# An attention backward loop emitted from two block programs, with dK and dV one unit later and three score banks in turn

## The chip, the cores and the metric

The kernel runs on one core of one Trainium2 chip. All times are device microseconds (us) of that core, from the first to the last instruction. One profiled execution of each kernel gives the trace; the times come from several executions. The engines are PE (TensorE: matmuls), ACT (ScalarE), DVE (VectorE) and POOL (GpSimd). The granted clock is the share of PE's full clock that the trace records as granted; a halving is a change of it from 1.0 to 0.5.

## The reference, cut to what matters

The program is a forward pass and the full vector-Jacobian product of one block: layer norm with modulation, attention with 32 heads of width 16 over 2048 tokens, then an MLP. Only the backward pass of the attention is touched:

```python
B, S, D, H = (1, 2048, 512, 32)                     # Dh = D // H = 16
def _A_ref(x, wqkv, wo):
    qkv = (x @ wqkv).reshape(B, S, 3, H, Dh).transpose(2, 0, 3, 1, 4)
    q, k, v = (qkv[0], qkv[1], qkv[2])
    scores = jnp.einsum('bhqd,bhkd->bhqk', q, k) * Dh ** (-0.5)
    p = _softmax(scores, axis=-1)
    o = jnp.einsum('bhqk,bhkd->bhqd', p, v)
    return o.transpose(0, 2, 1, 3).reshape(B, S, D) @ wo
# ... layer norms, modulation, MLP; then
_out, _vjp = jax.vjp(_f, A_x, A_wqkv, A_wo, B_w1, B_b1, B_w2, B_b2, c, w_mod)
_grads = _vjp(grad_out)
```

## The kernel before

The backward loop has 512 units. A unit is four heads, 128 queries and 512 keys; four units are a block. Per unit PE makes four scores (a 32-row tile of the array each), ACT their exponentials E, PE four products psD (32-row tiles again), DVE the two dS products, and PE a K quad and a V quad (four matmuls in four 32-column tiles, into accVK). dS is transposed by DMA, except for one unit in eight, whose tile is turned on PE and copied by ACT. After every sixteen units ACT copies accVK out (the vkb copy). Per block sixteen matmuls (dqacc) make dQ. All engines but POOL run in the order in which the loop emits.

```python
ework = ...tile_pool(name="phIe", bufs=4)            # E_u and dS_u
psd = ...tile_pool(name="psId", bufs=2, PSUM)        # psD, two banks each
pss = ...tile_pool(name="psIs", bufs=2, PSUM)        # two score banks
psx = ...tile_pool(name="psIx", bufs=1, PSUM)        # px (shared) and accVK

def score(u, hq, shared):                            # cut
    r = 32 * hq
    psS = psx.tile(..., tag="px") if shared else pss.tile(..., tag="ps")
    PE.matmul(psS[:], st["q"][r:r + 32, qt*P:(qt+1)*P], st["k"][r:r + 32, kc*512:kc*512+512],
              start=True, stop=True, tile_position=(r, 0))
    ACT.activation(bst[u][0][:, hq, :], psS[:], AF.Exp, scale=SCALE)

def k_quad(u):                                       # v_quad alike, with E_u and dOs_tok
    for hq in range(4):
        PE.matmul(cur["vk"][32*hq:32*hq+32, :], hst[hg]["qz"][:, qt, hq, :], bst[u][1][:, hq, :],
                  start=(qt == 0), stop=False, tile_position=(0, 32*hq), skip_group_check=True)

for j in range(2 * NU + 15):                         # half units
    u, pair, sub = j // 2, j % 2, j % 8
    for hi in range(2):
        i = 2 * sub + hi
        score(u, 2*pair + hi, i == 1 or (i in (4, 7) and not (j >= 8 and on_pe(j // 8 - 1))))
    if "turn" in held: ...                           # ACT copies the turned tile
    dp_pair((j - 1) // 2, (j - 1) % 2)               # two psD matmuls, one dS product on DVE
    if (j - 1) % 2 == 1: transpose_unit((j - 1) // 2)
    if 2 <= u < NU + 2:
        (k_quad if pair == 0 else v_quad)(u - 2)     # one quad in every half unit
    if sub in (1, 3) and on_pe(b): pe_turn(b, sub // 2)
    if sub in (5, 6): ...                            # two dq quads each
```

## Time and profile before

| | before |
|---|---|
| median time | 2749.24 us (3 runs, 2740.08 to 2750.76) |
| span of the profiled run | 2744.2 us |
| backward loop, first to last dS product | 1327.4 us, of 64 repeats of two blocks |
| mean granted PE clock, whole span | 0.897 |

The prediction below shows the slices, the loop's stretch, the groups and the timelines that it rests on. The first is the clock row of the page's 40 slices of before (tenths of the full clock); the second is a row of the groups, with busy time and mean ns behind the bar, then the idle time before it and what ended it:

```profile
PEclk8655569998998999787999999999999999999999
L1056 PE MATMUL psD_u<-iv,ido 32*128 32x512 bf16 x2048 | 406.6, 393 | 20.1 <-DMA ido<-dOT_st 14.3 <-DVE dS_u L1058 5.0
```

From slice 19 on, inside the loop, the clock is 9 tenths or more everywhere. In the stages ahead of it it is lower in places. A psD matmul then has a mean duration of 393 ns.

### The profile page before, as it was taken

How to read it: one execution, taken by the hardware profiler on the slowest of the kernel's cores; microseconds unless marked ns; L12 is line 12 of the kernel's file. 1: busy time of each engine (PE TensorE's matmuls, PEld its weight loads, DVE VectorE, ACT ScalarE, POOL GpSimd, SP SyncE). 2: the span in 40 equal slices, each digit the busy share in tenths (PEclk: the TensorE clock that was granted, in tenths of full speed). 3: DMA queues.
4: the chain of work that ended last, by engine and by line, in shares of the span. 5: the costliest groups of instructions: out<-in, count | busy, mean ns of one | idle time of the engine just before them, and what ended most of it. 6: DMA issues, size and time to landing. Idle time of an engine off the chain costs nothing.

```text
span 2744.2 us, 48487 instructions
## 1 busy us (share of the span) xinstructions
PE 2383.2 (87%) x18010; PEld 781.8 (28%) x18010; DVE 1763.4 (64%) x2232; ACT 2304.7 (84%) x3537; POOL 379.1 (14%) x378
## 2 busy tenths in 40 slices
PE   6799989888988988586898988988888989888899
PEld 2211123222322222232332333333233232332343
DVE  7101144435345443356988989989999898998973
ACT  4599999999999998202999999999999899998953
POOL 2000010211333133201011110101101011010100
PEclk8655569998998999787999999999999999999999
DMA  9863365346847656786999999999999999999982
GB/s 241 197 177 92 102 147 132 107 116 142 116 83 161 139 95 138 170 226 161 187 179 195 192 194 192 192 195 188 196 193 189 189 190 193 188 188 206 184 247 81
DMA packets 1271906, 459.69 MB, mean 168 GB/s; under 512 B 1152739, under 2 KB 1240807, under 8 KB 1271414
## 3 DMA queue, kind: packets, MB, share of 16 engines
q1 hardware_dynamic: 1254262, 425.42, 77.6%
q0 software_dynamic: 10944, 16.78, 4.2%
q10 hardware_dynamic: 6464, 14.40, 1.9%
q8 instruction: 142, 2.33, 0.3%
q14 instruction: 94, 0.77, 0.1%
HBM read 97.67 MB, written 74.47 MB: 63 GB/s over the span
## 4 chain that ended last, share of the span: by engine, by line
PE 27%; ACT 20%; DMA 4%; DVE 3%; issue 3%; SPq 1%; ACTq 1%; POOL 0%; DVEq 0%; POOLq 0%
ACT E_u L1046 15%; PE psS_u L1044 10%; PE accVK L1098 3%; ACT dsT L1157 3%; PE accVK L1089 3%; DVE dS_u L1058 2%; PE ptT L1079 2%; PE dqacc L1116 2%; PE pdh L1284 2%; PE pwq L1318 2%; DMA dsT<-dS_u 1%; PE psS_x L1044 1%; ACT dqtmp L1126 1%; PE psD_u L1056 1%; DMA part<-p_st 1%
## 5 line engine op out<-in xcount | busy, mean ns | idle before, releaser
L1058 DVE TENSOR_TENSOR dS_u<-psD_u,E_u 128x1024 bf16<-128x1024 f32 x1024 | 1196.4, 1217 | 146.8 <-PE psD_u L1056 88.9
L1046 ACT ACTIVATE E_u<-psS_u 128x512 bf16<-128x512 f32 x1790 | 990.8, 619 | 102.9 <-PE psD_u L1056 53.6
L701 ACT ACTIVATE ET<-psST 128x1024 bf16<-128x1024 f32 x1024 | 944.4, 1299 | 38.7 <-PE psST L699 37.7
L1044 PE MATMUL psS_u<-ik,iq 32*128 32x512 bf16 x1790 | 618.0, 386 | 106.2 <-ACT E_u L1046 64.7
L699 PE MATMUL psST<-qt_sb,kt_sb 32*128 32x512 bf16 x2048 | 408.3, 464 | 64.9 <-ACT ET L701 31.2
L1056 PE MATMUL psD_u<-iv,ido 32*128 32x512 bf16 x2048 | 406.6, 393 | 20.1 <-DMA ido<-dOT_st 14.3
L715 PE MATMUL oacc<-ET,vaug 128*32 128x512 bf16 x2048 | 247.5, 474 | 6.0 <-DVE ostage L719 6.0
L1044 PEld LDWEIGHTS <-iq 32*128 32x128 bf16 x2048 | 121.0, 91 | 342.2 <-issue 315.8
L1089 PE MATMUL accVK<-dS_u,qz 128*32 128x512 bf16 x2048 | 209.6, 398 | 3.0 <-DVE dS_u L1058 0.2
L1098 PE MATMUL accVK<-E_u,dOs_tok 128*16 128x512 bf16 x2048 | 205.4, 391 | 0.0
L699 PEld LDWEIGHTS <-kt_sb 32*128 32x128 bf16 x2048 | 90.0, 94 | 399.7 <-issue 388.6
L1131 POOL TENSOR_TENSOR dQacc<-dQacc,dqtmp 128x512 f32<-128x512 f32 x64 | 81.1, 1268 | 884.6 <-ACT dqtmp L1126 876.8
L1056 PEld LDWEIGHTS <-ido 32*128 32x128 bf16 x2048 | 105.1, 91 | 265.4 <-issue 262.4
L1046 ACT ACTIVATE E_u<-psS_x 128x512 bf16<-128x512 f32 x258 | 160.0, 620 | 14.8 <-PE psS_u L1044 14.6
L1116 PE MATMUL dqacc<-dsT,KS_tok 128*32 128x512 bf16 x2048 | 159.8, 390 | 12.2 <-ACT dsT L1157 12.2
L719 DVE COPY ostage<-oacc 128x512 f32<-128x512 f32 x32 | 22.0, 688 | 229.9 <-PE oacc L715 210.7
L376 DVE COPY part<-pm 128x512 f32<-128x512 f32 (+2 forms) x105 | 64.6, 615 | 150.7 <-PE pm L362 128.1
L1157 ACT ACTIVATE dsT<-ptT 128x1024 bf16<-128x1024 bf16 x128 | 134.4, 1050 | 1.1 <-PE ptT L1079 1.0
L715 PEld LDWEIGHTS <-vaug 128*32 128x32 bf16 x2048 | 54.9, 96 | 163.8 <-issue 163.8
L1044 PE MATMUL psS_x<-ik,iq 32*128 32x512 bf16 x258 | 100.4, 389 | 0.6 <-ACT E_u L1046 0.6
L1079 PE MATMUL ptT<-identb,dS_u 128*128 128x128 bf16 x1024 | 81.3, 224 | 11.6 <-ACT dsT L1157 11.4
L1089 PEld LDWEIGHTS <-qz 128*32 128x32 bf16 x2048 | 55.4, 93 | 123.3 <-issue 121.0
(262 smaller groups left out, 2104.1 us busy)
## 6 DMA issues: line engine op xcount, KB each, us to landing
p_st<-part POOLq DMA_DIRECT2D x36, 256.0 KB, 5.6
kt_sb<-qkT_st SPq DMA_DIRECT2D x128, 64.0 KB
wA<-in_B_w_dram SPq DMA_DIRECT2D x28, 256.0 KB
wB<-w1T_st SPq DMA_DIRECT2D x28, 256.0 KB
dsT<-dS_u SPq DMA_TRANSPOSE x448
wA<-w2T_st SPq DMA_DIRECT2D x21, 256.0 KB
wB<-in_B_w_dram SPq DMA_DIRECT2D x21, 256.0 KB
p_st<-part POOLq DMA_DIRECT2D x27, 192.0 KB, 4.2
```

What stands on the lines that cost most here:

```text
L699: PE.matmul(ps[:, hi, :], kt_sb[r:r + 32, kt * P:(kt + 1) * P], qt_sb[r:r + 32, :], start=True, stop=True, tile_position=(r, 0))
L701: ACT.activation(ET[:, 2 * pair:2 * pair + 2, :], ps[:], AF.Exp, scale=SCALE)
L715: PE.matmul(oacc[32 * hq:32 * hq + 32, :], lhsT, ET[:, hq, :], start=(kt == 0), stop=(kt == TT - 1), tile_position=(0, 32 * hq), skip_grou ...
L1044: PE.matmul(psS[:], st["q"][r:r + 32, qt * P:(qt + 1) * P], st["k"][r:r + 32, kc * 512:kc * 512 + 512], start=True, stop=True, tile_positi ...
L1046: ACT.activation(bst[u][0][:, hq, :], psS[:], AF.Exp, scale=SCALE)
L1056: PE.matmul(psD[:, hi, :], st["do"][r:r + 32, qt * P:(qt + 1) * P], st["v"][r:r + 32, kc * 512:kc * 512 + 512], start=True, stop=True, til ...
L1058: DVE.tensor_tensor(dS_u[:, 2 * pair:2 * pair + 2, :], psD[:], E_u[:, 2 * pair:2 * pair + 2, :], ALU.mult)
L1079: PE.transpose(pt[:, i, :], held["dS"][:, 2 * half + i // 4, kt * P:(kt + 1) * P], identb[:])
L1089: PE.matmul(cur["vk"][32 * hq:32 * hq + 32, :], hst[hg]["qz"][:, qt, hq, :], bst[u][1][:, hq, :], start=(qt == 0), stop=False, tile_positi ...
L1098: PE.matmul(acc[32 * hq:32 * hq + DH, :], dOs_tok[:, qt, (hg * 4 + hq) * DH:(hg * 4 + hq + 1) * DH], E_u[:, hq, :], start=False, stop=(qt ...
L1116: PE.matmul(acc[32 * hq:32 * hq + 32, :], KS_tok[:, kc * 4 + kt, h * DH:h * DH + 32], tT[:, :, hq * 4 + kt, :], start=(kt == 0), stop=(kt ...
L1157: ACT.activation(dst, pt[:], AF.Identity)
```

## The change

The intent was to take three waits out of the loop: scores that wait for exponentials (a third bank for every score), dS products that wait behind the dK/dV work (quads one unit later), and dS products that wait for the transposing DMA (a fifth E and dS buffer). For that the loop over half units became two strings of marks, one for blocks that turn a tile on PE and one for the others: `s` score, `e` exponential, `D` psD pair with its dS product, `q` a K or V quad, `t`/`T` turn and copy, `d`/`Q` dQ matmuls and their copy out.

```diff
-        ework = ph.enter_context(tc.tile_pool(name="phIe", bufs=4))
+        ework = ph.enter_context(tc.tile_pool(name="phIe", bufs=5))
-        pss = ph.enter_context(tc.tile_pool(name="psIs", bufs=2, space=bass.MemoryType.PSUM))
+        banks = {"A": "ps0", "B": "ps1", "C": "px"}
     ... (score and expo become two functions, dq_out is split from dq_quad)
+        order_t = (
+            "s0 q s1 e0 e1 D s2 q s3 e2 D s4 q e3 s5 s6 D "
+            "e4 e5 t1 q e6 s7 D s8 T1 s9 e7 e8 s10 e9 D s11 e10 "
+            "t2 q e11 T2 s12 e12 s13 D e13 D q d1 d2 s14 D Q s15 "
+            "e14 q q e15 ").split(), "ACBACBAABCABABBA"
+        order_n = (
+            "q s0 e0 s1 D q s2 e1 D e2 s3 q s4 e3 D s5 d1 "
+            "e4 e5 d2 s6 D s7 Q q q e6 e7 q s8 e8 D s9 q "
+            "e9 s10 s11 D e10 q e11 s12 e12 s13 D e13 s14 s15 D e14 e15 ").split(), "CBACBABACBACBACB"
-            for j in range(2 * NU + 15):
-                ... (one fixed program, one quad in each half unit)
+            nD, nq = -1, -6
+            for b in range(NU // 4 + 3):
+                toks, bank = order_t if on_pe(b - 1) else order_n
+                for tok in toks:
+                    ... (one branch for each mark; q counts quads from nq, D pairs from nD)
```

The number of matmuls, exponentials, products and transposes stays the same. What moves is where the quads stand. Before, every half unit had one; the strings have them in bunches: `Q q q e6 e7 q` in the middle of `order_n`, then only two `q` up to its end.

## The prediction

> **What bounds the kernel now.** I read the page's slices first, to find the stretch that the change touches, then one stretch view of it, the groups, and last the timelines of two engines inside it. In the slices each digit is a fortieth of the 2744.2 us span:

> ```profile
> PE   6799989888988988586898988988888989888899
> DVE  7101144435345443356988989989999898998973
> ACT  4599999999999998202999999999999899998953
> DMA  9863365346847656786999999999999999999982
> ```

> From slice 19 to slice 38 four resources are busy at once. That is the backward attention loop: the group of dS products starts at 1286.6 us and its last one at 2612.8. The stretch view over just that time (columns: length, then busy time of PE, weight load, DVE, ACT, POOL, then granted clock, DMA share, GB/s):

> ```profile
> 1286.60:2612.80 1326.20, 1189.62 (x11200) 402.89 (x11196) 1195.17 (x1024) 1241.66 (x2327) 138.47 (x101) 0.97 1.10 191
> ```

> The loop is 1326.2 us, 48% of the kernel, and nothing outside it is edited. It is 64 repeats of two blocks of four units (512 units), so one repeat takes 1326.2 / 64 = 20.72 us. No engine fills it: DVE lacks 131 us, ACT 85, PE 137. The groups over that time say what ended their waits:

> ```profile
> L1058 DVE TENSOR_TENSOR dS_u<-psD_u,E_u 128x1024 bf16<-128x1024 f32 x1024 | 1196.4, 1217 | 146.8 <-PE psD_u L1056 88.9 <-ACT vkb L1101 17.4 <-DMA dsT<-dS_u 16.9
> L1046 ACT ACTIVATE E_u<-psS_u 128x512 bf16<-128x512 f32 x1787 | 989.2, 619 | 72.3 <-PE psD_u L1056 53.6 <-PE psS_u L1044 13.4 <-DVE dS_u L1058 1.1
> L1044 PE MATMUL psS_u<-ik,iq 32*128 32x512 bf16 x1787 | 617.1, 386 | 103.9 <-ACT E_u L1046 63.1
> ```

> The circle is in the last two rows: a score matmul waits for an exponential to leave a bank, and the exponential waits for PE. DVE is outside the circle and starves for psD, which PE issues in order behind a blocked score. DVE's timeline shows where:

> ```profile
> 1893.99 15.24 DVE L1058 TENSOR_TENSOR dS_u<-psD_u,E_u 128x1024 bf16<-128x1024 f32 x13 [0.66 <-PE psD_u L1056]
> 1909.55 1.22 DVE L1058 TENSOR_TENSOR dS_u<-psD_u,E_u 128x1024 bf16<-128x1024 f32 x1 [0.32 <-PE accVK L1098]
> 1911.19 1.22 DVE L1058 TENSOR_TENSOR dS_u<-psD_u,E_u 128x1024 bf16<-128x1024 f32 x1 [0.42 <-ACT vkb L1101]
> 1912.64 1.23 DVE L1058 TENSOR_TENSOR dS_u<-psD_u,E_u 128x1024 bf16<-128x1024 f32 x1 [0.23 <-PE psD_u L1056]
> 1914.55 16.52 DVE L1058 TENSOR_TENSOR dS_u<-psD_u,E_u 128x1024 bf16<-128x1024 f32 x14 [0.68 <-PE psD_u L1056]
> ```

> Thirteen or fourteen products run without a gap, then there are 1.3 to 1.7 us of gaps, all in the block that also turns a dS tile on PE and copies it out on ACT. Starts inside a dense run are (16.52 - 1.23) / 13 = 1.176 us apart, so sixteen cost about 18.8. ACT just after that:

> ```profile
> 1915.79 1.65 ACT L1046 ACTIVATE E_u<-psS_u 128x512 bf16<-128x512 f32 x3
> 1917.34 0.59 ACT L1046 ACTIVATE E_u<-psS_x 128x512 bf16<-128x512 f32 x1
> 1917.82 1.09 ACT L1046 ACTIVATE E_u<-psS_u 128x512 bf16<-128x512 f32 x2
> 1918.77 0.63 ACT L1046 ACTIVATE E_u<-psS_x 128x512 bf16<-128x512 f32 x1
> ```

> Three exponentials from the two psS_u banks alone are (1.65 - 0.59) / 2 = 0.53 us apart. Where the third bank (psS_x) is mixed in, 1917.34 to 1917.82 and two more to 1918.77 give 0.48 and 0.475. This is the clearest support for the third bank. 32 exponentials at 0.53, two 1024-wide copies at 0.90 (start to next start), two dQ copies at 0.49 and half a vkb copy make 17.0 + 1.8 + 1.0 + 0.25 = 20.0, close to the 20.2 to 20.6 between the repeats.

> [...] two psD matmuls start together, and the next kind starts about 0.32 us after, while 8 dqacc matmuls of one mode take 0.54 to the next kind, 0.27 per quad.

> **The change, part by part.** No arithmetic, transfer or instruction count changes: 2048 score matmuls, 2048 exponentials, 1024 dS products, 448 transposes through DMA and 128 copies of turned tiles stay.

> (1) Three score banks in turn, in a fixed string per block. The exponential goes from 0.53 to 0.48 apart where two banks had to do. ACT's floor per repeat: 32 x 0.477 + 2 x 0.905 + 2 x 0.485 + 0.25 = 18.3 us. This bank is still shared with the turned tiles and dQ, six uses in one block and five or six in the other.

> (2) Two programs. The turning block costs ACT 16 x 0.477 + 1.81 + 0.49 = 9.9 us against 8 x 1.17 = 9.4 of DVE; the other costs 8.1. So ACT falls behind by 0.6 and wins 1.2 back. The strings put scores and exponentials far enough ahead of the D marks to carry that. I followed the turning block by hand: the third D waits on DVE for a psD pair, the first turn is behind it, the copy behind that (0.6 later), then five exponentials, and the thirteenth or fourteenth score before the sixth D. That brings the sixth D to the first D + 6.2 us where DVE could do it at 5.85. So 0.35 us of gap stays per repeat.

> (3) dK and dV one unit later. Their quads no longer wait for fresh dS, and the vkb copy sits between the last dV quad and dQ work, so most of the 17.4 us for vkb should go.

> (4) The fifth E and dS pair. It gives the transposing DMA 2.4 us more before DVE needs the buffer: most of the 16.9 us goes, if the DMA keeps up.

> (5) PE only changes order. Fewer switches between score mode and quad mode, so it should stay under 18 us per repeat.

> DVE's floor is 16 x 1.17 = 18.7; with 0.35 left in (2) and about 0.1 for vkb, 19.1 to 19.2.

> **The DMA.** The queue's own view of transposes in a crowded piece:

> ```profile
> 1771.33 12.38 SPq L1069 DMA_TRANSPOSE dsT<-dS_u  x5
> ```

> That is 2.48 us each, 17.3 for the seven of a repeat, with the loads of the next head and stores of dV and dQ on top. The other estimate: 191 GB/s x 20.72 us = 3.96 MB per repeat, and the best 20 us stretches move 202 to 209 GB/s, so 18.9 to 19.6 us if that is the most it can do. DMA is as close a bound as DVE. Two near-equal bounds with random arrival do not give the larger one, but somewhat more: I choose 19.45 us per repeat.

> Sum: (20.72 - 19.45) x 64 = 81 us, minus 1 to 2 us for the longer drain. From 2749 this gives 2670 us, 2.9% faster.

> **Rivals.** *The DMA takes DVE's place.* For it: share 1.10, digit 9 in every slice of the loop. Against it: the transposing queue waited for DVE before nearly each issue, and only 16.9 us of DVE's waits are DMA's. If its ceiling is 195 GB/s, a repeat takes 20.3 and only 27 us are won (2722), and dS waits for DMA would grow beyond 60 us.
> *PE blocks on the shared bank.* The px bank now carries scores, turns and dQ in a fixed order, so one late copy stops the whole in-order PE. For it: ptT and dqacc already wait for the dsT copy some 23 us. It would leave 0.7 to 1 us of gaps per repeat: about 2710.
> *Everything overlaps.* DVE dense at 18.7: 64 x 2.0 = 128 us, 2621. Against it: (2) by hand, and the DMA.
> *The strings are tuned for average durations.* If a DMA-late tile shifts the phases, the fixed order may serialise, and nothing is won: 2745. I see little for it.

> **Range and chances.** 19.0 to 20.15 us per repeat gives 2640 to 2715. Two per cent is 55 us, a repeat of 19.86, on the near side of my estimate by 0.4 us, about one of my standard deviations. Faster by over 2%: 0.74; within: 0.23; slower: 0.03.

> **What would show it.** In the new profile the loop's stretch should be 1230 to 1260 us, with DVE at 95 to 97% of it; the dS product's wait for psD below 35 us (from 88.9), for vkb below 6; scores waiting for exponentials below 30 (from 63.1); exponentials with starts 0.48 apart in all banks; busy times of each instruction unchanged. GB/s should rise to about 203. The prediction is wrong if dS waits for DMA grow past 40 us, if GB/s stays at 191, or if psD remains DVE's releaser at over 60 us.

The 32-row and the 32-column forms of PE's tiles are what it calls modes. No term of the sum is cut: it came to (20.72 - 19.45) x 64 = 81 us, less 1 to 2 for the drain, and so to 2670 us. The 19.45 us is the author's estimate, from DVE's 1.176 us per product and from DMA stretches of 202 to 209 GB/s.

## The result, and the profile after

The change made the kernel slower. A ratio here is the mean time of one kernel's fast runs over the mean of the other's in the same rounds, so it is not quite the ratio of the medians.

| | before | after |
|---|---|---|
| median of the comparison | 2748.48 us (4 runs) | 2856.77 us (4 runs, 2852.96 to 2863.25) |
| ratio | | 1.0402, 95% interval 1.0373 to 1.0432 |
| loop, first to last dS product | 1327.4 us | 1433.7 us |
| rest of the span | 1416.8 us | 1422.5 us |
| mean granted clock, whole span | 0.897 | 0.776 |

Nearly all of the time (106 of 112 us) went into the loop. The page's slices of after:

```profile
PE   6799989889888894868999999999999999999999
DVE  6101153454435353457888888888888888888873
PEclk9655579988997997886777777777777777777799
```

From slice 19 on, inside the loop, PE shows 9 everywhere, DVE fell to 8, and the clock row, which had 9s there, has 7s up to the loop's end. The stretch view of the loop says the same (length, busy time of PE, weight load, DVE, ACT, POOL, then clock, DMA share, GB/s):

```profile
1291.00:2724.60 1433.60, 1398.30 (x11209) 393.12 (x11204) 1201.97 (x1024) 1252.92 (x2327) 138.82 (x101) 0.73 1.01 177
```

PE was busy 1189.62 us for the same matmuls before and is busy 1398.30 us now, 97.5% of the stretch, at a clock of 0.73 instead of 0.97. The groups of after:

```profile
L1060 DVE TENSOR_TENSOR dS_u<-psD_u,E_u 128x1024 bf16<-128x1024 f32 x1024 | 1202.0, 1220 | 246.7 <-PE psD_u L1058 179.8
...
L1058 PE MATMUL psD_u<-iv,ido 32*128 32x512 bf16 x2048 | 533.4, 482 | 15.3 <-DMA ido<-d_st 13.9
...
L1040 PE MATMUL psS_A<-ik,iq 32*128 32x512 bf16 x768 | 369.0, 480 | 13.9 <-ACT E_u L1046 3.8
```

Two things stand side by side here. The waits at which the change aimed did go: scores of bank A wait for exponentials 3.8 us (bank B 0.9) instead of 64.7 in the whole span before, and the releasers that follow psD for the dS products are now other PE matmuls (psS_B 29.6, psS_A 15.1), no longer the vkb copy or the transposing DMA. But DVE waits for psD twice as long, 179.8 us, because each psD matmul now takes 482 ns instead of 393. PE's matmuls became slower (psD 482 ns, scores of bank A 480), not one wait.

**When the clock falls.** The granted clock in the loop has two values only, 1.0 and 0.5, and it changes once per repeat: full for 10.2 us, half for 10.2 or 13.7. In both traces every stretch of one value but the last, at the trace's end, has a whole multiple of 3.413 us (63 of before's 64 clock records, 175 of after's 176). So I cut one repeat along that grid (same columns as the stretch view above):

```profile
1859.90:1863.30 3.40, 3.40 (x43) 0.90 (x34) 3.40 (x4) 2.86 (x6) 0.00 (x0) 1.00 1.10 210
1863.30:1866.70 3.40, 3.28 (x44) 1.06 (x42) 3.40 (x4) 3.23 (x8) 0.00 (x0) 1.00 1.44 96
1866.70:1870.10 3.40, 3.09 (x25) 0.79 (x21) 3.40 (x4) 3.40 (x8) 0.00 (x0) 1.00 1.28 240
1870.10:1873.50 3.40, 3.40 (x23) 0.49 (x20) 3.18 (x4) 2.99 (x7) 0.00 (x0) 0.50 1.05 215
1873.50:1876.90 3.40, 3.40 (x25) 1.20 (x22) 1.87 (x3) 2.62 (x5) 0.00 (x0) 0.50 1.19 214
1876.90:1880.40 3.50, 3.44 (x24) 1.14 (x21) 2.23 (x2) 3.28 (x7) 0.00 (x0) 0.50 0.81 155
1880.40:1883.80 3.40, 3.40 (x30) 0.83 (x32) 2.46 (x3) 2.29 (x5) 0.00 (x0) 0.50 0.88 174
```

Read the first bracket in each line, PE's matmuls. In the third window they drop from 43 and 44 to 25, four of which only start at its very end. PE is still busy 3.09 of 3.40 us, 91%, and DVE and ACT are full, so nothing looks wrong; yet the clock is halved from the next window on. At half clock PE is busy nearly all the time (98% or more in 225 of after's 228 such windows), with 23 to 25 matmuls listed per window, and DVE (third busy time) falls from 3.40 to 1.87. After a window with 30, thanks to dQ work, the clock comes back (it is 1.00 in the window that follows these). PE's timeline inside the third window:

```profile
1867.24 0.37 PE L1040 MATMUL psS_C<-ik,iq 32*128 32x512 bf16 x1
1867.24 0.39 PE L1058 MATMUL psD_u<-iv,ido 32*128 32x512 bf16 x2
1867.56 0.39 PE L1100 MATMUL accVK<-E_u,dOs_tok 128*16 128x512 bf16 x4
1867.89 0.39 PE L1040 MATMUL psS_B<-ik,iq 32*128 32x512 bf16 x1
1868.22 0.37 PE L1040 MATMUL psS_A<-ik,iq 32*128 32x512 bf16 x1
...
1868.71 0.37 PE L1040 MATMUL psS_C<-ik,iq 32*128 32x512 bf16 x1
1869.20 0.37 PE L1040 MATMUL psS_B<-ik,iq 32*128 32x512 bf16 x1
...
1870.46 0.60 PE L1040 MATMUL psS_C<-ik,iq 32*128 32x512 bf16 x1
```

This is the second half of `order_n`: after 1867.56 no quad comes for over 2 us. Single scores start 0.49 us apart, at the pace of ACT's exponentials, which hold the three banks, and each fills a 32-row tile, a quarter of the array, for 0.37 us. PE is occupied by tiny work. The last line has the same matmul at half clock, 0.60 us. Of the 63 windows that precede a halving in after, 61 are like this one: two quads start in them, and no turn. The quads alone (accVK matmuls in the first bracket), after and then before:

```profile
1859.90:1863.30 3.40, 1.62 (x20) 0.00 (x0) 1.00 1.10 210
1863.30:1866.70 3.40, 0.96 (x16) 0.00 (x0) 1.00 1.44 96
1866.70:1870.10 3.40, 0.76 (x12) 0.00 (x0) 1.00 1.28 240
```

```profile
1902.50:1905.90 3.40, 1.19 (x12) 0.00 (x0) 1.00 1.39 143
1905.90:1909.30 3.40, 1.00 (x12) 0.00 (x0) 1.00 1.14 176
1909.30:1912.70 3.40, 0.82 (x12) 0.65 (x1) 1.00 1.24 256
```

A matmul across a window's edge is listed in both. Counted by starts, after has 20, 16 and 8, before 12, 12 and 8, with eight matmuls of a turn in the last; the six windows of this repeat of before have 24 to 32 matmuls in all, those of after 21 to 43 at full clock.

**A reckoning over all windows.** I counted, from the trace's records of matmul starts and of the clock, how much of the array each 3.41 us window used: each matmul with its streaming time times its part of the array. Scores, psD and quads stream 512 columns through a 32-row or 32-column tile, a quarter of the array; transposes 128 columns through all of it; so each counts the same: 0.216 us x 1/4 = 0.054 us at full clock, twice that at half. (The times are from start to start, from the trace of before. The qkv matmuls of L235, 512 columns on the whole array, start 215 or 216 ns after the one before them in 150 of 164 cases at full clock, and 426 or 427 ns in 19 of 25 at half. The four matmuls of a quad start 2 to 5 ns apart, and a dQ quad follows another after 215 or 216 ns in all 240 cases at full clock, so that four quarter tiles together take what one matmul on the whole array takes. Transposes of 128 columns start 55 or 56 ns apart in 775 of 851 cases, and 106 or 107 ns in 38 of 45 at half clock.) V quads have only 16 active columns (`128*16` in the timeline) and are counted by the 32-column tile that they occupy. The result in the loop:

| window at full clock, followed by | before: windows, share of the array used | after |
|---|---|---|
| half clock | 6, at most 0.369 | 63, between 0.327 and 0.363 |
| full clock | 360, from 0.355, median 0.45 | 127, from 0.410, median 0.63 |

PE's busy share does not tell them apart: 0.91 to 0.94 ahead of a halving in after, while 5% of before's untroubled windows had 0.83 or less. The share of the array does: in a recount of both traces (559 windows, those at the loop's edges included) a line at 0.37 misplaces one. That is some 23 such matmuls in 3.41 us (0.37 x 3.41 / 0.054). For the way back, the 71 windows at half clock that were followed by full clock had 0.74 to 0.95 of the half rate, all but one 0.78 or more, and the 177 others at most 0.77. That is 0.37 to 0.39 of the full rate: about the same amount of array work. Before runs at 176 matmuls x 3.41 / 20.72 = 29 per window, so it lies some 20% above that line on average and evenly so; after has the same average and bunches it.

### The profile page after: what moved, and what is told of

Same layout as the page of the kernel before. It is cut to its first block, busy times and chain, and to the rows that moved or that the text cites. A ratio compares the mean times of both kernels' runs of the same rounds, so it can differ in the third digit from the quotient of the medians.

```text
span 2856.2 us, 48399 instructions
## 1 busy us (share of the span) xinstructions
PE 2594.1 (91%) x17939; PEld 772.7 (27%) x18010; DVE 1769.7 (62%) x2232; ACT 2316.3 (81%) x3537; POOL 379.3 (13%) x378
## 4 chain that ended last, share of the span: by engine, by line
PE 45%; ACT 8%; DVE 3%; DMA 2%; issue 1%; SPq 1%; another core or an unknown queue 0%; ACTq 0%; POOL 0%; POOLq 0%; DVEq 0%
ACT E_u L1046 7%; PE psS_A L1040 7%; PE accVK L1100 6%; PE dqacc L1118 6%; PE accVK L1091 6%; PE psS_B L1040 4%; PE ptT L1081 4%; PE psS_C L1040 4%; PE psD_u L1058 3%; DVE dS_u L1060 2%; PE pdh L1305 2%; PE pwq L1339 1%; DMA part<-p_st 1%; SPq L325 0%; PE pm L516 0%
## 5 line engine op out<-in xcount | busy, mean ns | idle before, releaser
L1060 DVE TENSOR_TENSOR dS_u<-psD_u,E_u 128x1024 bf16<-128x1024 f32 x1024 | 1202.0, 1220 | 246.7 <-PE psD_u L1058 179.8
L1058 PE MATMUL psD_u<-iv,ido 32*128 32x512 bf16 x2048 | 533.4, 482 | 15.3 <-DMA ido<-d_st 13.9
L1046 ACT ACTIVATE E_u<-psS_A 128x512 bf16<-128x512 f32 x768 | 484.5, 631 | 55.1 <-DMA rows_st<-racc 32.0
L1046 ACT ACTIVATE E_u<-psS_B 128x512 bf16<-128x512 f32 x768 | 483.6, 630 | 27.6 <-PE psD_u L1058 26.8
L1040 PE MATMUL psS_A<-ik,iq 32*128 32x512 bf16 x768 | 369.0, 480 | 13.9 <-ACT E_u L1046 3.8
L1040 PE MATMUL psS_B<-ik,iq 32*128 32x512 bf16 x768 | 364.8, 475 | 8.6 <-ACT E_u L1046 0.9
L1046 ACT ACTIVATE E_u<-psS_C 128x512 bf16<-128x512 f32 x512 | 326.3, 637 | 24.2 <-PE psD_u L1058 22.4
L1100 PE MATMUL accVK<-E_u,dOs_tok 128*16 128x512 bf16 x2048 | 240.4, 460 | 0.0
L1091 PE MATMUL accVK<-dS_u,qz 128*32 128x512 bf16 x2048 | 239.9, 459 | 0.0
L1040 PE MATMUL psS_C<-ik,iq 32*128 32x512 bf16 x512 | 229.6, 448 | 6.7
L1188 ACT ACTIVATE dsT<-ptT 128x1024 bf16<-128x1024 bf16 x128 | 131.0, 1024 | 33.2 <-PE ptT L1081 33.0
L1058 PEld LDWEIGHTS <-ido 32*128 32x128 bf16 x2048 | 104.3, 95 | 128.8 <-issue 119.8
L1081 PE MATMUL ptT<-identb,dS_u 128*128 128x128 bf16 x1024 | 132.2, 309 | 0.2 <-DVE dS_u L1060 0.2
```

Of the source, the lines that this page charges most:

```text
L1040: PE.matmul(psS[:], st["q"][r:r + 32, qt * P:(qt + 1) * P], st["k"][r:r + 32, kc * 512:kc * 512 + 512], start=True, stop=True, tile_positi ...
L1046: ACT.activation(bst[u][0][:, hq, :], sst.pop((u, hq))[:], AF.Exp, scale=SCALE)
L1058: PE.matmul(psD[:, hi, :], st["do"][r:r + 32, qt * P:(qt + 1) * P], st["v"][r:r + 32, kc * 512:kc * 512 + 512], start=True, stop=True, til ...
L1060: DVE.tensor_tensor(dS_u[:, 2 * pair:2 * pair + 2, :], psD[:], E_u[:, 2 * pair:2 * pair + 2, :], ALU.mult)
L1081: PE.transpose(pt[:, i, :], held["dS"][:, 2 * half + i // 4, kt * P:(kt + 1) * P], identb[:])
L1091: PE.matmul(cur["vk"][32 * hq:32 * hq + 32, :], hst[hg]["qz"][:, qt, hq, :], bst[u][1][:, hq, :], start=(qt == 0), stop=False, tile_positi ...
```

## The experiments

Three theories. **Starving**: a window in which the array does too little at full clock halves the clock, and the half clock, which cannot make up for it, is the loss. **Load**: the clock falls because PE's work has become denser, so more work in the array lowers it further. **Order**: the fixed order of the strings serialises PE and ACT, and the clock only accompanies it. Loop lengths below run from first to last dS product; half-clock time is within the loop, from the clock records. All results were correct. The ratios between 0.98 and 1 are gains under the 2% mark; their intervals leave out 1 except for a1's.

| kernel | median us (range) | before, same rounds | ratio (95%) | loop us | half clock us, in stretches |
|---|---|---|---|---|---|
| after | 2856.77 (2852.96–2863.25) | 2748.48 | 1.0402 (1.0373–1.0432) | 1433.7 | 782 in 64 |
| a1_spread_plain | 2741.40 (2738.77–2750.67) | 2745.32 | 0.9986 (0.9964–1.0008) | 1323.3 | 258 in 46 |
| a2_spread_both | 2714.72 (2707.96–2718.22) | 2745.32 | 0.9881 (0.9857–0.9906) | 1293.6 | 159 in 33 |
| a3_filler | 2784.81 (2783.58–2788.4) | 2745.32 | 1.0140 (1.0124–1.0156) | 1367.3 | 282 in 63 |
| a4_filler_turn | 2702.56 (2700.14–2711.41) | 2749.51 | 0.9839 (0.9820–0.9859) | 1279.0 | 74 in 9 |
| b1_starve | 2884.83 (2877.07–2903.94) | 2745.32 | 1.0512 (1.0471–1.0554) | 1463.1 | 518 in 70 |
| b2_bufs5 | 2738.48 (2727.37–2739.52) | 2750.74 | 0.9944 (0.9915–0.9973) | 1317.5 | 53 in 5 |
| b3_late5 | 2731.83 (2729.99–2734.07) | 2750.74 | 0.9931 (0.9904–0.9957) | 1305.6 | 39 in 3 |
| c1_even | 2805.46 (2800.8–2810.61) | 2750.74 | 1.0197 (1.0171–1.0223) | 1383.1 | 402 in 59 |
| c2_even_bufs4 | 2838.91 (2837.8–2844.77) | 2750.74 | 1.0322 (1.0298–1.0347) | 1419.1 | 444 in 60 |
| c3_by_time | 2701.66 (2699.39–2708.42) | 2749.51 | 0.9836 (0.9818–0.9853) | 1278.5 | 87 in 12 |
| c4_by_time_late | 2710.58 (2706.37–2714.2) | 2749.51 | 0.9862 (0.9845–0.9879) | 1285.1 | 102 in 14 |

(Before itself: loop 1327.4 us, 70 us at half clock in 6 stretches.)

**a1_spread_plain**: after, with two quads of `order_n` moved from its middle to its starved second half; nothing else. (The expectation speaks of three; the edit moves two.)

```diff
-            "e4 e5 d2 s6 D s7 Q q q e6 e7 q s8 e8 D s9 q "
-            "e9 s10 s11 D e10 q e11 s12 e12 s13 D e13 s14 s15 D e14 e15 "
+            "e4 e5 d2 s6 D s7 Q q e6 e7 s8 e8 D s9 q "
+            "e9 s10 s11 D e10 q e11 s12 e12 s13 D q e13 s14 s15 D e14 q e15 "
```

> The changed kernel with three of its eight dK/dV quads moved later inside the plain block only: the three quads in a row become one, and two stand between the last four exponentials. Nothing is added or removed. Starving theory (the clock is halved after a 3.41 us window in which the PE array does too little at full clock, which in the changed kernel is always the second half of the plain block): the halvings in the loop fall from 62 to under 20, the granted clock of the loop rises from 0.73 to over 0.93, and the time falls from 2857 to between 2640 and 2720 us. Load theory (the clock falls because the loop gives PE more work per microsecond): the work is the same, so the clock stays at 0.70 to 0.77 and the time within 1% of 2857. Order theory (the fixed PE order serialises, the clock is a companion): the time moves by at most 2% either way and the clock stays below 0.8.

Measured: 115 us faster than after, level with before. Its loop in the stretch view:

```profile
1293.00:2616.30 1323.30, 1260.08 (x11209) 389.67 (x11208) 1186.58 (x1024) 1218.99 (x2328) 138.87 (x101) 0.90 1.10 191
```

The same 11209 matmuls take 138 us less busy time, and the clock is 0.90 instead of 0.73. The halving in the plain block is gone. The 46 left are short (27 are one window of 3.41 us), and 45 of them follow windows of the turning block that contain part of a turn, with a median share of 0.36. So the starving theory had the direction right and its size wrong: it expected under 20 halvings, a clock above 0.93 and at most 2720 us. The forecasts of the other two (a clock below 0.8, a time within 2% of 2857) fail. Moving two marks in a string of over forty is enough, so the clock is not a constant to which the order is indifferent. The order theory is not yet excluded: the edit changes the order as well.

**a2_spread_both**: a1 and, in `order_t`, one quad from behind `t2` to behind `e8`.

```diff
-            "e4 e5 t1 q e6 s7 D s8 T1 s9 e7 e8 s10 e9 D s11 e10 "
-            "t2 q e11 T2 s12 e12 s13 D e13 D q d1 d2 s14 D Q s15 "
+            "e4 e5 t1 q e6 s7 D s8 T1 s9 e7 e8 q s10 e9 D s11 e10 "
+            "t2 e11 T2 s12 e12 s13 D e13 D q d1 d2 s14 D Q s15 "
```

> As the run before, and one quad of the turning block moved forward from behind the second turn to the middle between both turns. Starving theory: the turning block between its two turns is the next window near the limit, so this run has no more halvings than the one before and a time equal to it or up to 20 us less, if the first run still shows some; if the first shows none, the two are the same within 0.5%. Load and order theories: as before, within 2% of 2857 us, clock below 0.8.

Measured: 27 us below a1 (up to 20 had been forecast), and 1.2% below before. Half-clock time fell from 258 to 159 us. Of the halvings that are left, 24 follow windows with one quad and part of a turn.

**a3_filler**: after's own order, plus 256 useless matmuls on the whole array in the second half of the plain block; the score overwrites what they write, so the results stay right.

```diff
+            if u // 4 % 2 == 1 and u % 4 >= 2 and hq % 2 == 1:
+                PE.matmul(psS[:], st["q"][:, qt * P:(qt + 1) * P], st["k"][:, kc * 512:kc * 512 + 512], start=True, stop=True)
             PE.matmul(psS[:], st["q"][r:r + 32, ...        # the score, unchanged
```

> The changed kernel in its own order with 256 useless full-array matmuls added (four in each plain block, before every second score of its second half, into the bank that the score then overwrites; the result is unchanged). Each costs PE about 0.3 us at full clock with its mode switches, 77 us of PE in all. Starving theory: the sparse window gets 0.86 us more of full-array work, its share rises from 0.33 to over 0.5, the clock rises to over 0.9, and the kernel becomes faster for added work: 2660 to 2760 us. Load theory: more work, a lower clock or the same, 2857 to 2960 us. Order theory: 256 x 0.3 to 0.6 us more on a PE that is already 98% busy, 2930 us or more.

(Its 0.3 us for a useless matmul is an estimate, as is that of a4 below; in the PE timeline of after above, a quad and the 32-row tiles before and behind it start 0.32 to 0.33 us apart.)

Measured: PE has 256 x 0.216 = 55 us more to stream, and the kernel is 72 us faster than after. In the stretch view:

```profile
1287.20:2654.50 1367.30, 1318.49 (x11464) 409.81 (x11461) 1197.64 (x1024) 1249.90 (x2328) 138.56 (x101) 0.90 1.06 185
```

More matmuls (x11464 instead of x11209), less busy time, a higher clock. This excludes load, and order too: the order of all useful work is that of after, and both theories expected 2857 us or more. It did not bring everything back (the starving theory had 2660 to 2760 us), because the halving moved: all 63 now follow windows with part of a turn, in the block that got no filler.

**b1_starve**: the other way round. In the kernel before, with its two banks and its own program, the quads of half units 7 and 0 are held back and issued at half unit 1.

```diff
+            late = []
-                    (k_quad if pair == 0 else v_quad)(u - 2)
+                    late.append((k_quad if pair == 0 else v_quad, u - 2))
+                if sub not in (7, 0) or u >= NU:
+                    while late:
+                        f, v = late.pop(0)
+                        f(v)
```

> The other way round, on the kernel before: the dK/dV quads of the last and the first half unit of each block are held back and issued together with the quad of the second half unit, so that some 2.9 half units (3.7 us) pass without a quad. Nothing is added or removed, both score banks stay two. Starving theory: windows that fall into this stretch do less than 0.3 of the array's work, the clock of the loop drops from 0.97 to below 0.85 in this kernel as well, and the time rises from 2748 to 2800 us or more. Load theory: less dense PE work, the clock stays above 0.95. Order theory: at most 1% slower, from psD being late once per block, with the clock above 0.95.

```profile
1289.80:2752.80 1463.00, 1262.23 (x11212) 390.68 (x11210) 1210.47 (x1024) 1254.30 (x2328) 138.22 (x101) 0.82 0.99 173
```

Measured: 5.1% slower than before, with 70 halvings instead of 6 and a clock of 0.82. The windows ahead of the halvings have a median share of 0.35 and at most 0.38; the expectation, under 0.3, was too low. None of the strings, banks or buffers of the change is in this kernel. Holding quads back costs something in itself, which this run does not separate from the clock; that bunching makes the clock fall, it shows.

**b2_bufs5**: before with a fifth E and dS buffer. **b3_late5**: the fifth buffer and the quads one unit later, in before's program.

```diff
-        ework = ph.enter_context(tc.tile_pool(name="phIe", bufs=4))
+        ework = ph.enter_context(tc.tile_pool(name="phIe", bufs=5))      # b2 and b3
-                if 2 <= u < NU + 2:
-                    (k_quad if pair == 0 else v_quad)(u - 2)
+                if 3 <= u < NU + 3:                                      # b3 only
+                    (k_quad if pair == 0 else v_quad)(u - 3)
```

> The kernel before with a fifth E and dS buffer and nothing else. The prediction gave this part most of the 16.9 us that dS products wait for DMA: 5 to 17 us faster than 2748, clock unchanged (above 0.95 in the loop). If buffers are not what holds those products, under 5 us.

> The kernel before with five buffers and its quads one unit later, still one quad per half unit and two score banks. The starving theory expects no change of the clock, as the quads stay evenly spread: 5 to 30 us faster than 2748 (dS waits for DMA and vkb gone). If lateness of the quads by itself starved the array, the clock of the loop would fall below 0.9 and the time rise above 2770.

Measured: 0.56% and 0.69% faster than before; by medians 12 and 19 us. The dS group of b2 (that of b3 names psD with 85.6 us and vkb with 19.7):

```profile
L1058 DVE TENSOR_TENSOR dS_u<-psD_u,E_u 128x1024 bf16<-128x1024 f32 x1024 | 1198.6, 1219 | 133.8 <-PE psD_u L1056 91.4 <-ACT vkb L1101 19.5 <-ACT E_u L1046 4.1
```

With five buffers the DMA is no longer named (16.9 us before), and about that much is won. Later quads alone do not remove the wait for the vkb copy, 19.7 us; in after, where it went, the order around the copy differs as well. Quads spread as before keep the clock: 5 and 3 halvings.

**c1_even**: after with the quads spread by count over the `D` marks, six in `order_t` and ten in `order_n`.

```diff
-            "s0 q s1 e0 e1 D s2 q s3 e2 D s4 q e3 s5 s6 D e4 e5 t1 q e6 s7 D s8 T1 s9 e7 e8 s10 e9 D s11 e10 "
-            "t2 q e11 T2 s12 e12 s13 D e13 D q d1 d2 s14 D Q s15 e14 q q e15 "
+            "s0 q s1 e0 e1 D s2 q s3 e2 D s4 q e3 s5 s6 D e4 e5 t1 e6 s7 D s8 T1 s9 e7 e8 q s10 e9 D s11 e10 "
+            "t2 e11 T2 s12 e12 s13 D e13 q D d1 d2 s14 D Q s15 e14 q e15"
     ... (order_n: ten quads, about one after each D)
-            nD, nq = -1, -6
+            nD, nq = -1, -5
```

> The changed kernel with its sixteen dK/dV quads per repeat spread by a count: every three product intervals in a row (3.5 us) hold at least four quads' worth of array work, a turn or two dQ quads counted as two; the quads start one place earlier. Banks, buffers, D marks and turns are as in the changed kernel. Starving theory: no window in the steady loop is under the limit, so the halvings fall from 62 (31 with the earlier spread) to the few [...] as in the kernel before (under 12); granted clock of the loop 0.95 or more; loop 1235 to 1275 us; kernel 2640 to 2690 us, where the prediction had put the change. If the clock is up and the time is still above 2700, the rest is DMA or the shared bank. Load theory: more work per microsecond than in any run so far, the clock falls below 0.85 and the time is above 2720.

```profile
1289.10:2672.20 1383.10, 1310.64 (x11211) 379.37 (x11207) 1196.24 (x1024) 1232.20 (x2328) 138.69 (x101) 0.85 1.05 183
```

Measured: 2% slower than before, clock 0.85, 59 halvings with a median share of 0.34. This was a miss, and an instructive one. Even by count is not even by time: around `t2` ACT makes the two copies `T1` and `T2`, 0.90 and 0.91 us from start to next start (at 1704.56 and 1707.85 us of c1), so that part of the string lasts longer than its marks suggest, and between the turns it was left with one quad; 48 of the 59 windows have one quad and part of a turn. The halvings went with the work per 3.41 us, not per mark.

**c2_even_bufs4**: c1 with four buffers.

```diff
-        ework = ph.enter_context(tc.tile_pool(name="phIe", bufs=5))
+        ework = ph.enter_context(tc.tile_pool(name="phIe", bufs=4))
```

> The evenly spread version with four E and dS buffers again. If the fifth buffer carries what the prediction gave it: dS waits for DMA and exponentials wait for E buffers, 15 to 60 us slower than the evenly spread version with five. If the fifth buffer is worth nothing: within 0.5% of it.

Two of the exponential groups of c2:

```profile
L1046 ACT ACTIVATE E_u<-psS_A 128x512 bf16<-128x512 f32 x768 | 477.5, 622 | 70.3 <-PE accVK L1100 34.1 <-DMA rows_st<-racc 30.6 <-PE psD_u L1058 3.7
...
L1046 ACT ACTIVATE E_u<-psS_C 128x512 bf16<-128x512 f32 x512 | 318.9, 623 | 53.5 <-PE psD_u L1058 28.8 <-PE accVK L1100 20.4 <-PE psS_B L1040 1.2
```

Measured: 33 us slower than c1. Exponentials wait 34.1 + 20.4 = 54.5 us for V quads, which hold the E buffer: with the quads a unit later the fifth buffer is needed. In this order it is worth more than the 12 us of b2.

**a4_filler_turn**: a2 plus 192 useless matmuls on the whole array in the turning block, where a2's last halvings came from.

```diff
+            if u // 4 % 2 == 0 and (u % 4, hq) in ((2, 0), (2, 2), (3, 0)):
+                PE.matmul(psS[:], st["q"][:, qt * P:(qt + 1) * P], st["k"][:, kc * 512:kc * 512 + 512], start=True, stop=True)
```

> The version with the earlier spread (2715 us, 31 halvings, nearly all after a window of the turning block with one quad and one turn) with 192 useless full-array matmuls added: three in each turning block, around and behind the second turn, where PE waits for ACT; the result is unchanged. They cost up to 0.3 us of PE each, 58 us in all, in time that PE mostly has idle there. Starving theory: the windows concerned rise from 0.34 to about 0.5, the halvings fall below 12, and the kernel gets faster by added work, 2650 to 2705 us. Load theory: no fewer halvings, 2715 to 2775 us. The evenly counted version was a miss of mine (2805 us: it left one quad between the two turns, where ACT's copies stretch the interval); that miss is in line with the starving theory only if filling this very place helps.

Measured: halvings go from 33 to 9 and half-clock time from 159 to 74 us. With 192 x 0.216 = 41 us more to stream, the median is 12 us lower (ratio to before 0.9839 against 0.9881). The ends of the two intervals overlap slightly, so the gain in time is likely and not certain; that the added work cost nothing is plain. The loop of a4:

```profile
1287.30:2566.30 1279.00, 1224.50 (x11339) 406.31 (x11399) 1174.40 (x1024) 1214.48 (x2328) 138.74 (x101) 0.97 1.15 198
```

PE is busy 1224.50 us although it has more to do; in a2 it was 1229.41, at a clock of 0.94. (The weight loads show all the 192 added matmuls, x11399 where a2 has x11207; the matmul records only 128 of them. Some are missing from the trace.)

**c3_by_time**: after with its quads spread roughly evenly by time instead of by marks; nothing added. **c4_by_time_late** is the same with `nq = -8`, the quads two half units later still.

```diff
+            "s0 q s1 e0 e1 D s2 q s3 e2 D s4 q e3 s5 s6 D e4 e5 t1 q e6 s7 D s8 q T1 s9 e7 e8 q s10 e9 D s11 e10 "
+            "t2 q e11 T2 s12 e12 s13 D e13 D d1 d2 s14 D Q s15 e14 q e15"                                # order_t
+            "s0 e0 s1 D q s2 e1 D e2 s3 q s4 e3 D s5 d1 e4 e5 d2 s6 D s7 Q q e6 e7 s8 q e8 D s9 e9 q s10 "
+            "s11 D q e10 e11 s12 e12 q s13 D e13 s14 s15 D q e14 e15"                                    # order_n
```

> The sixteen quads of a repeat spread by time and not by count: three between the two turns, one behind the second, three at the head of the turning block, six in the second half of the plain block, so that every 3.4 us hold four quads' worth. Nothing added, same banks, marks and buffers, quads' numbering as in the changed kernel. Starving theory: few halvings (under 15), granted clock of the loop over 0.94, 2640 to 2700 us, faster than both kernels. If quads before the first turn copy delay it and ACT becomes the bound, the clock is up and the time 2700 to 2740. Load theory: 2720 us or more with a clock below 0.9.

> As the version spread by time, each quad one unit later in its numbering, so that the vkb copy falls at the end of the turning block where PE has passed its quad. Starving theory: the same halvings as the version spread by time. If vkb's place costs ACT 0.3 us every second repeat: 5 to 10 us faster than it; if later quads hold E buffers too long: slower by 10 us or more, with exponentials waiting for quads.

Measured: c3 is 1.64% faster than before (2701.66 us, just above the forecast's 2700) and beats both kernels; against after that is 155 us by medians, from the places of the `q` marks alone. c4 is 9 us slower, so still later quads bring nothing. The loop of c3 and its dS group:

```profile
1289.50:2567.90 1278.40, 1198.83 (x11211) 406.31 (x11207) 1173.68 (x1024) 1215.96 (x2328) 138.89 (x101) 0.97 1.14 198
```

```profile
L1060 DVE TENSOR_TENSOR dS_u<-psD_u,E_u 128x1024 bf16<-128x1024 f32 x1024 | 1173.8, 1214 | 121.0 <-PE psD_u L1058 83.3 <-PE psS_A L1040 16.5 <-PE psS_B L1040 12.7
```

The clock is that of before, 0.97, and PE's busy time is within 10 us of before's.

**What the runs settle.** Taking the starved windows away without adding work (a1, a2, c3), filling them with useless work (a3, a4) and making them in the old kernel (b1) all move the clock as the starving theory says, and the time with it. Over all thirteen traces there are 443 windows followed by a halving and 3694 that were not. With transposes and fillers counted whole and the other matmuls as quarters, a line at 0.37 of the array misplaces 52 of these 4137. With the quarter tiles counted as halves the best line misplaces 175; counted whole, 190; with V quads counted by their 16 active columns, 246; and a line through PE's busy share, in place of the reckoning, misplaces 345 at best. A plain count of matmuls is a near rival, since all but the fillers weigh the same here; it misplaces 108, and only a3 and a4 tell the two apart. (The last four counts are from a recount over the same traces, in which the line at 0.37 misplaces 49.) With transposes counted as a quarter the best line misplaces 183, with transposes left out 187. In the traces of before and after alone, 559 windows with 70 halvings, the same counts are 1 for the line at 0.37, then 51 (halves), 69 (whole), 8 (16 columns), 67 (busy share), 5 (plain count), and 69 for transposes either way. All this is a reckoning from these traces: it says which way of counting separates their windows. How the clock is decided, no trace shows.

## Why the prediction was wrong

It gave 2670 us and 74% for faster by over 2%; the kernel came out 4% slower, far outside the range.

**Step (5), "PE only changes order … so it should stay under 18 us per repeat", is the step that failed.** PE's busy time per repeat was 1189.62 / 64 = 18.6 us before, so over 18 already in the stretch view that the prediction shows, and is 1398.30 / 64 = 21.8 us after. The step took the duration of a matmul for fixed, since the loop's clock was 0.97. At one clock it was: a psD matmul takes 384 ns on average in before and 386 in after at full clock, 595 and 607 at half. But 888 of after's 2048 are at half clock, and only 88 of before's; and where the quads stand decided that (a1, c3). The prediction listed the quads' move as step (3) and priced only the waits it would remove. No rival named the clock; the nearest, strings tuned for averages that serialise, foresaw no gain but no loss either, and had the wrong cause, since a3 keeps the order and gains 72 us. Its list of what would show it right, "busy times of each instruction unchanged", did point to the place: 393 ns became 482.

The size follows from the windows, as an estimate: counted by starts, a half-clock window of after takes 21.8 matmuls on average where the loop needs 29, so it costs (29 - 21.8) / 29 x 3.4 = 0.8 us. After has 782 / 3.41 / 64 = 3.6 such windows per repeat: 3.0 us. Its 3.0 windows at full clock per repeat take 32.6 and win about 1.3 us back. That leaves 1.7 us, by which its repeat of 1433.7 / 64 = 22.40 us is longer than before's 20.72. This is bookkeeping and no further proof; against c3, with 1278.5 / 64 = 19.98, the repeat is 2.4 us longer.

**Steps (1) and (4) had their mechanisms right; (3) is not shown.** After's exponentials run 0.48 us apart in all banks, at full clock, and scores of banks A and B wait only 3.7 us for exponentials in c3's loop too, where the clock is 0.97. But the 0.53 us of step (1) came from one stretch: over before's loop the median spacing within the two banks is 0.49, so the third bank saves less per exponential than the step has. The fifth buffer alone brought 12 us of the "most of the 16.9" (b2). For (3) the later quads alone did not remove the wait for vkb (19.7 us in b3); it went only together with the new order.

**The sum was too large as well.** With the clock kept at 0.97, c3 shows what the mechanism is worth: about 48 us by the medians instead of 81, a repeat of 19.98 us instead of 19.45. In c3 dS still waits 83.3 us for psD, where the prediction had less than 35, so step (2), which left 0.35 us of gaps per repeat, is mis-sized: (1278.40 - 1173.68) / 64 = 1.6 us of DVE's idle time per repeat are left. Why is open. DMA moves 198 GB/s in c3's loop, as much as in any run here, and the prediction's rival of an assumed ceiling near 195 GB/s (20.3 us per repeat) is close to what c3 does; but its sign, dS waits for DMA beyond 60 us, is missing (at most 5.7 us). Of the rival of a blocked shared bank c3 shows little: bank C's scores wait 8.3 us for the turned tile's copy. No run separates the transposing queue from the order of PE.

**What the prediction could have seen.** The clock records of before have the values 1.0 and 0.5 only, in multiples of 3.41 us. Before's page already showed 5s and 6s in its clock row, outside the loop, and six halvings lay inside it. A change that moves quarter-array matmuls about should have counted matmuls per window, before and after.
